# Writing out the order of the transfer queue for the whole attention stage, with a third buffer for the raw weight loads and a second one for decoded words

## The chip, the cores and the metric

The kernel runs on one core of one Trainium2 chip. The metric is device time in microseconds (us) of one execution; lower is better. Kernels are compared by the median of several executions.

The five engines have queues of their own, each worked off in order: TensorE (PE; its weight loads, PEld, overlap its matmuls), VectorE (DVE), ScalarE (ACT), GpSimd (POOL) and SyncE (SP). In this kernel nearly every DMA is issued by SP, so a DMA that has to wait for its data or for a free buffer holds up all DMAs behind it in SP's order. "Landing" is the time from a DMA's issue to the arrival of its data.

## What is computed

Three stages follow one another: an attention whose keys are masked by cluster, a dense layer with a rational activation, and a soft mixture of experts.

```python
q_assign = np.argmax(np.einsum('bhsd,hcd->bhsc', q_n, c_n), axis=-1)      # 2 x 8 heads, 768 tokens, 64 wide, 16 clusters
k_assign = np.argmax(np.einsum('bhsd,hcd->bhsc', k_n, c_n), axis=-1)
mask = q_assign[:, :, :, None] == k_assign[:, :, None, :]
scores = np.where(mask, scale * np.matmul(q, k.transpose(0, 1, 3, 2)), -1e9)
attn = softmax(scores);  x = attn @ v                                     # -> 1536 tokens x 512
h = x @ w_in                                                              # w_in 512 x 2048
g = (a0 + a1 h + a2 h^2 + a3 h^3) / (1 + |b0||h| + |b1| h^2)
y = g @ w_out                                                             # w_out 2048 x 512
out = soft_moe(y, phi, w1, w2)                                            # 8 experts, 4 slots each
```

`w_in` and `w_out` come to the core as 64-bit floats. [...]

## The kernel before

The attention works on 8 pairs of heads. A pair has 12 **slots**, one for each head and block of 128 queries, 96 slots in all (`NSL`), and a loop over the slots writes every engine's instructions out in order. In slot n PE turns the probabilities of unit n (`turn`, L349) and copies of them are made on ACT (`turned`, L355); PE computes the scores of unit n+2 (`a1_mm`, L325 and L326), DVE scales them and takes their minimum (`a1_neg`, L334), ACT exponentiates them in the next slot (`a1_exp`, L338), and PE adds some products with v (`a2_av`, L362). A unit of scores waits for a PSUM buffer that DVE's L334 of the unit before sets free, so DVE and PE follow each other closely.

Two other kinds of work are spread over the slots by a plan: a dictionary from slot to engine key to a list of functions, filled by `add(slot, steps)` and emptied by `run(slot, keys)`.

*Preparing a pair* (`prep`). The pair after next has its cluster scores computed (L216), the best cluster of every token found (L231 to L246), the masks made on ACT (`masks`, L256), k split into a high and a low part on POOL (`ksplit`, L266 and L269) and q likewise (`qsplit`, L284 and L285). The parts are then spread over operand tiles by DMAs from SBUF to SBUF: four of `ka` (L273), two of `kb` (L276), six of `qh` and `ql` (L293), eight small ones of the mask rows `nh` (L261).

*Decoding the weights* (`decode_steps`). There are 32 decodes: the even ones of blocks of `w_in`, the odd ones of `w_out`. Decode i is due at slot `DEC[i] = 2 + 53*i//20`, one in every 2.65 slots. Its steps: three slots ahead a DMA brings the raw words into `raw64[i % 2]` (L475); at slot DEC two DVE operations take them apart (`bits`, L481 and L482), the first readers of the raw words; one slot later ACT and DVE go on (L485, L488); two slots later DVE reads the raw words for the last time (`sign`, L492); three slots later POOL multiplies (`value`, L497) into `w`, of which there is one buffer. For an odd decode `w` is stored at once (L501) and PE works on it from slot +4 (L522); for an even one POOL splits it at slot +4 (`parts`, L506 and L507) and stores both parts (L508). The dense layer reads these stores back.

What sets the order: PE, ACT, DVE and POOL run in the order that the code writes out (`manual_schedule`). SP does so up to slot 12 (`SP_FREE`); from there on the scheduler of the language places SP's DMAs. Pair 1 is prepared in the first slots by a table of its own (`PREP1`, one slot for every step left in `prep`'s list).

After the attention come the dense layer (`h_mm`, L741 to L744, with weights loaded at L573) and the experts (weights loaded at L721), which the change leaves as they are.

Of the kernel before, what the change touches and what calls it, by code (L numbers as in the profile page):

```python
# [8 lines left out]
F32 = mybir.dt.float32  # L9
F32R = mybir.dt.float32r  # L10
BF16 = mybir.dt.bfloat16
I32 = mybir.dt.int32
# [40 lines left out]
def tile_kernel(ctx, tc, qT, kT, v, cenT, cenP, consts, constsb, ab, w_in, w_out, phi, w1, w2, out, dbg=None):  # L53
    nc = tc.nc
    PE, ACT, DVE, POOL, SP = nc.tensor, nc.scalar, nc.vector, nc.gpsimd, nc.sync

    B, NPB, _, S = qT.shape
    H = 2 * NPB
    D = v.shape[4]
    NP = B * H // 2  # L60
    HS = S // 2
# [50 lines left out]
    NBUF = 2  # L112

    LEAD = 2
    SP_FREE = 12

    PREP1 = (0, 0, 1, 1, 2, 3, 3, 4, 5, 6)

    OPENW = 4
    ops = [[{n: att.tile([128, S], F32R, name=f"{n}_{i}_{h}") for n in ("q1", "q2", "k1", "k2")}  # L120
# [10 lines left out]
    def load_v(p):  # L131
        b, hp = divmod(p, H // 2)
        vs[p] = v_p.tile([128, 2, 6, D], F32, tag="v", name="vt")
        SP.dma_start(vs[p], v[p])
# [6 lines left out]
    def first_pair(r, o, f):  # L141

        hold = f["hold"]
        w0 = slice(0, HS)
        ms = {}

        def q_split():
            qh, ql = (t_p.tile([128, S], F32R, tag=n, name=n) for n in ("qh", "ql"))
            hold["qh"], hold["ql"] = qh, ql
            ACT.copy(qh[:, w0], r["q"][:, w0])  # L150
            DVE.tensor_tensor(ql[:, w0], r["q"][:, w0], qh[:, w0].bitcast(F32), ALU.subtract)

        def rows(name, h):
            g = 2 * (name == "k") + h
            m = ms[name, h] = m_tile(BF16)
            oh = hold["eq"].rearrange("p i (c g) n -> p i c g n", c=2)
            for c in range(2):
                for i in range(3):
                    j = (3 * c + i) * 128
                    PE.transpose(m[64:80, j:j + 128], oh[:, i, c, g, :], identb)  # L160

        def q_rows(h, c):
            w = slice(c * HS, (c + 1) * HS)
            DVE.tensor_scalar(o[h]["q2"][64:80, w], ms["q", h][64:80, w], -1.0, None, ALU.add)

        def k_rows(h):
            ACT.activation(o[h]["k2"][64:80, :], ms["k", h][64:80, 0:S], AF.Copy, scale=BIG)

        def front(nxt):
            f["scores"]()  # L170
            q_split()
            f["ksplit"](0)
            for h in range(2):
                f["qspread"](h, w0)
            f["ksplit"](1)
            f["scaled"]()
            f["scT"]()
            f["best"](0)
            f["best"](1)
            for i in range(3):  # L180
                f["first"](i)
            idle(11)
            for h in range(2):
                rows("k", h)
                k_rows(h)
                rows("q", h)
                q_rows(h, 0)
            nxt[0]()
            idle(1)
            nxt[1]()  # L190

        def back(nxt):
            nxt[2]()
            idle(3)

        rest = [(0, "G", lambda: f["qsplit"](1)),
                (1, "D", lambda: q_rows(0, 1)),
                (2, "D", lambda: q_rows(1, 1))]
        return front, back, rest

    def prep(p):
# [3 lines left out]
        o = ops[p % NBUF]  # L205
# [47 lines left out]
        def masks():  # L253

            nh = tile_(t_p, "nh", [128, HS], F32R)
            ACT.activation(nh, hold.pop("mo")[:, 0:HS], AF.Identity, bias=cst[:, C_OFF:C_OFF + 1], scale=cst[:, C_SCL:C_SCL + 1])  # L256
            for h in range(2):
                for c in range(2):
                    w = slice(c * HS, (c + 1) * HS)
                    for n, at in (("q2", 64 * c + 16 * h), ("k2", 64 * c + 32 + 16 * h)):  # L260
                        SP.dma_start(o[h][n][64:80, w].bitcast(F32), nh[at:at + 16, :].bitcast(F32))  # L261

        def ksplit(i):
            if i == 0:
                ka, kb = tile_(t_p, "ka", [128, S], F32R), tile_(t_p, "kb", [128, S], F32R)
                POOL.tensor_scalar(ka, r["k"], 1.0, 1.0, ALU.mult, ALU.mult)  # L266
                for c in range(2):
                    w = slice(c * HS, (c + 1) * HS)
                    POOL.tensor_tensor(kb[:, w], r["k"][:, w], ka[:, w].bitcast(F32), ALU.subtract)  # L269
                for h in range(2):  # L270
                    a = slice(64 * h, 64 * h + 64)
                    for dst in (o[h]["k1"][0:64, :], o[h]["k1"][64:128, :]):
                        SP.dma_start(dst.bitcast(F32), ka[a, :].bitcast(F32))  # L273
            else:
                for h in range(2):
                    SP.dma_start(o[h]["k2"][0:64, :].bitcast(F32), hold["kb"][64 * h:64 * h + 64, :].bitcast(F32))  # L276

        def qsplit(c, done=None):
            if "qh" not in hold:
                tile_(t_p, "qh", [128, S], F32R)  # L280
                tile_(t_p, "ql", [128, S], F32R)
            qh, ql = hold["qh"], hold["ql"]
            w = slice(c * HS, (c + 1) * HS)
            POOL.tensor_scalar(qh[:, w], r["q"][:, w], 1.0, 1.0, ALU.mult, ALU.mult)  # L284
            POOL.tensor_tensor(ql[:, w], r["q"][:, w], qh[:, w].bitcast(F32), ALU.subtract)  # L285
            if c == 1:
                for h in range(2):
                    qspread(h, slice(HS, S) if p == 0 else slice(0, S))

        def qspread(h, w):  # L290
            a, l = slice(64 * h, 64 * h + 64), slice(64 - 64 * h, 128 - 64 * h)
            for dst, src in ((o[h]["q1"][a, w], hold["qh"]), (o[h]["q1"][l, w], hold["ql"]), (o[h]["q2"][0:64, w], hold["qh"])):
                SP.dma_start(dst.bitcast(F32), src[a, w].bitcast(F32))  # L293

        if p == 0:
# [6 lines left out]
            (4 + b, "D0", lambda: best(0)),  # L302
            (4 + b, "D0", lambda: best(1)),
            (5 + b, "D0", lambda: first(0)),
            (8, "G", lambda: (ksplit(0), ksplit(1))),
            (6 + b, "D0", lambda: first(1)),
            (7 + b, "D0", lambda: first(2)),
            (7 + b, "P", ohT),
            (8 + b, "A", masks),
            (11, "G", lambda: qsplit(0)),  # L310
            (12, "G", lambda: qsplit(1)),
        ]

    nvs, sums, s1s, es = {}, {}, {}, {}
# [147 lines left out]
    w_in2 = dram.tile([NF, 128, 2, NCC, 128], F32, name="w_in2")  # L462
    w_out32 = dram.tile([4, 128, 4, 512], F32, name="w_out32")

    raw64 = [dec_p.tile([128, 3, 172, 2], I32, name=f"raw64{i}") for i in range(2)]
    for t in raw64:
        POOL.memset(t.rearrange("p r n t -> p (r n t)")[:, 1024:1032], 0)

    def decode_steps(i, src, dst, after=None):

        hold = {}
        raw = raw64[i % 2]

        def dma():
            SP.dma_start(raw.rearrange("p r n t -> p (r n t)")[:, 0:1024], src)  # L475
# [17 lines left out]
                                     ALU.bitwise_and, ALU.bitwise_or)  # L493

        def value():
            w = dec_p.tile([128, 516], F32, tag="w", name="w")
            POOL.tensor_tensor(w.rearrange("p (r n) -> p r n", r=3), hold["mh"].bitcast(F32), hold["ex"].bitcast(F32),  # L497
                               ALU.mult)
            w = hold["w"] = w[:, 0:512]
            if after:  # L500
                SP.dma_start(dst, w)  # L501

        def parts():
            w = hold["w"]
            w2 = dec_p.tile([128, 2, 512], F32R, tag="w2", name="w2")
            POOL.tensor_scalar(w2[:, 0, :], w, 1.0, 1.0, ALU.mult, ALU.mult)  # L506
            POOL.tensor_tensor(w2[:, 1, :], w, w2[:, 0, :].bitcast(F32), ALU.subtract)  # L507
            SP.dma_start(dst, w2.rearrange("p a n -> p (a n)").bitcast(F32))  # L508

        return [(-3, "S", dma), (0, "D1", bits), (1, "A", expo), (1, "D1", mant), (2, "D1", sign),  # L510
                (3, "G0", value)] + (after(hold) if after else [(4, "G", parts)])

    wph = {}
    DEC = [2 + 53 * i // 20 for i in range(2 * NF)]
# [69 lines left out]
    def add(slot, steps):  # L584
        for off, eng, fn in steps:
            plan.setdefault(slot + off, {}).setdefault(eng, []).append(fn)

    def run(slot, engines):
        for eng in engines:
            for fn in plan.get(slot, {}).pop(eng, []):  # L590
                fn()
# [1 line left out]
    for g in range(2 * NP):  # L593
        add(6 * g + 6, norm(g))
    for i, d in zip(DEC, decs):
        late = i == DEC[4]
        add(i, [(max(o + (late and e == "S"), -LEAD - i), e, fn) for o, e, fn in d])
    engines = {mybir.EngineType.PE, mybir.EngineType.Activation, mybir.EngineType.DVE, mybir.EngineType.Pool}
    manual = tc.manual_schedule(engines=engines | {mybir.EngineType.SP})
    manual.__enter__()  # L600
# [11 lines left out]
    pend = None  # L612
    for n in range(-LEAD, NSL + 6):
        p, k = divmod(n, 12)
        if n == SP_FREE:
            manual.__exit__(None, None, None)
            manual = tc.manual_schedule(engines=engines)
            manual.__enter__()
        if n == -LEAD:
            run(-1, ("S",))  # L620
        if n == 0:
            run(1, ("S",))
            load_v(0)
            load(2, "k")
        if n == 1:
            load(2, "q")
        if n == 2:
            load_v(1)
        if k == 4 and n > 0 and p + 2 < NP:
            add(n, prep(p + 2))  # L630
        if k == 6 and 0 < p < NP - 1:
            load_v(p + 1)
        if n > 0 and k == 0 and p + 2 < NP and p:
            load(p + 2, "q")
# [11 lines left out]
        if n == NSL - 8:  # L646
            DVE.tensor_scalar(ncoef, coef, -1.0, None, ALU.mult)
            DVE.tensor_tensor(babs, coef[:, 4:6], ncoef[:, 4:6], ALU.max)
        run(n, ("D0", "D", "D1", "D2", "G0", "S", "G"))
        if 0 <= n < NSL:  # L650
            turn(n)
        if pend is not None:
# [665 lines left out]
```

## Time and profile before

| | |
|---|---|
| median of 3 runs | 546.82 us (545.81 to 548.43) |
| the profiled execution | 547.18 us |
| its span, first to last instruction | 545.3 us |
| attention, first to last L334 | 18.26 to 295.39 us |
| DMA engines busy, 18.26 to 269.14 us | 0.75 |

The numbers that follow come from the one profiled execution, 0.36 us above the median; 1.9 us of it lie outside its span. "Busy" is the time covered by an engine's instructions; ends of matmuls are modelled. The granted clock of TensorE (PEclk) is a share of full speed: it has two levels, 1.2 and 2.4 GHz, and 0.55 says that nearly all of a stretch went at the lower one. In the page and the answers L334 is line 334 of the kernel before.

### The profile page before, as it was taken

Reading aid. Unit: us, or ns where it says so; the run is one execution under the profiler, and the core shown is the slowest. Engines: PE = TensorE matmul, PEld = TensorE weight load, DVE = VectorE, ACT = ScalarE, POOL = GpSimd, SP = SyncE. Lnnn points to the kernel's source line nnn. Section 1 sums busy time; section 2 is a strip of 40 time slices with the busy share of each in tenths; the row PEclk is TensorE's granted clock in tenths of the full one; section 3 lists DMA queues with packets and bytes.
Section 4 is the critical chain, followed back from the end, with each engine's and each line's share of the span. In section 5 each row is a group of like instructions: output and inputs, shape, how many; then the busy total and the mean of one; then the engine's idle time right before and its main releaser. Section 6 shows DMA issues by size and latency. Waiting matters only on the chain.

```text
span 545.3 us, 9828 instructions
## 1 busy us (share of the span) xinstructions
PE 511.0 (94%) x3446; PEld 340.8 (62%) x3446; DVE 404.3 (74%) x746; ACT 362.9 (67%) x646; POOL 275.0 (50%) x315
## 2 busy tenths in 40 slices
PE   8898959989899799799999999999999999999994
PEld 3555637656556466566666687777677776765362
DVE  5678858879788588787864299999979997986022
ACT  2576746878677578678777388877678885873111
POOL 3260954945757649546542475555466544561000
PEclk9998988999989899989999999999999999999998
DMA  7988776695785777867531277766477655789997
GB/s 225 261 195 246 202 207 228 187 284 179 214 259 160 215 237 208 240 195 217 169 117 40 77 256 278 245 226 218 169 289 251 231 201 187 288 316 401 422 416 301
DMA packets 44944, 126.18 MB, mean 231 GB/s; under 512 B 7136, under 2 KB 9696, under 8 KB 40288
## 3 DMA queue, kind: packets, MB, share of 16 engines
q1 hardware_dynamic: 44752, 125.31, 70.3%
q8 instruction: 27, 0.44, 0.3%
q10 hardware_dynamic: 144, 0.26, 0.1%
q14 instruction: 21, 0.17, 0.1%
HBM read 89.56 MB, written 15.73 MB: 193 GB/s over the span
## 4 chain that ended last, share of the span: by engine, by line
PE 60%; DMA 20%; DVE 8%; SPq 5%; ACT 4%; issue 2%; POOL 0%; ACTq 0%; DVEq 0%; POOLq 0%
PE h L741 8%; PE h L744 8%; PE av L362 8%; PE h L742 8%; PE sT L349 7%; DMA raw<-w_in 5%; DMA raw<-w_out 4%; PE s L325 4%; DMA wt<-w 4%; DVE e L334 3%; PE s L326 3%; PE gt L788 3%; DMA rawk<-kT 3%; PE pf L1153 3%; SPq L261 2%
## 5 line engine op out<-in xcount | busy, mean ns | idle before, releaser
L338 ACT ACTIVATE e<-e,nv 128x768 f32<-128x768 f32 x96 | 89.9, 937 | 68.5 <-DVE e L334 62.8
L334 DVE TENSOR_SCALAR_CACHE_REDUCE e<-s 128x768 f32<-128x768 f32 x96 | 91.5, 954 | 36.0 <-PE s L326 28.4
L325 PE MATMUL s<-k,q 128*128 128x384 f32 x192 | 75.1, 391 | 18.9 <-DVE e L334 18.5
L349 PEld LDWEIGHTS sT<-cst,e 128*128 128x128 f32 x576 | 62.0, 142 | 48.8 <-ACT eT L355 23.9
L349 PE MATMUL sT<-cst,e 128*128 128x128 f32 x576 | 84.5, 283 | 3.2 <-ACT eT L355 2.7
L497 POOL TENSOR_TENSOR w<-mh,ex 128x516 f32<-128x516 f32 x32 | 41.2, 1286 | 87.1 <-DVE ex L492 32.4
L355 ACT COPY eT<-sT 128x768 f32<-128x768 f32 x96 | 75.3, 784 | 11.4 <-PE sT L349 11.2
L741 PE MATMUL h<-xh,w 128*128 128x512 f32 x192 | 80.6, 420 | 0.4 <-DMA w<-w_in 0.4
L362 PE MATMUL av<-eT,vt 128*64 128x384 f32 x384 | 80.7, 524 | 0.0
L742 PE MATMUL h<-xl,w 128*128 128x512 f32 x192 | 75.3, 392 | 0.0
L758 POOL TENSOR_SCALAR q<-u,babs 128x512 f32<-128x512 f32 x47 | 36.2, 771 | 74.5 <-ACT u L756 74.5
L326 PE MATMUL s<-k,q 80*128 80x384 f32 x192 | 66.8, 348 | 0.8 <-DMA k<-kb 0.6
L760 POOL TENSOR_TENSOR q<-q,u 128x512 f32<-128x512 f32 x47 | 60.9, 1296 | 3.8
L744 PE MATMUL h<-xh,w 128*128 128x512 f32 x192 | 52.9, 396 | 0.0
L325 PEld LDWEIGHTS s<-k,q 128*128 128x128 f32 x192 | 37.1, 193 | 24.7 <-DVE e L334 24.1
L756 ACT ACTIVATE u<-h 128x512 f32<-128x512 f32 x47 | 27.9, 594 | 28.5 <-PE h L744 28.1
L741 PEld LDWEIGHTS h<-xh,w 128*128 128x128 f32 x192 | 36.1, 188 | 16.9 <-DVE r L774 6.7
L759 DVE TENSOR_TENSOR p<-p,h 128x512 f32<-128x512 f32 x47 | 32.1, 683 | 15.0 <-ACT p L757 14.9
L744 PEld LDWEIGHTS h<-xh,w 128*128 128x128 f32 x192 | 36.0, 188 | 8.5
L742 PEld LDWEIGHTS h<-xl,w 128*128 128x128 f32 x192 | 36.2, 189 | 6.8 <-issue 0.5
L481 DVE TENSOR_SCALAR ex<-raw 128x516 int32<-128x516 int32 x32 | 21.8, 681 | 23.0 <-DMA raw<-w_in 11.3
L766 ACT ACTIVATE r<-q,epsc 128x512 f32<-128x512 f32 x47 | 32.8, 698 | 9.0 <-POOL q L760 7.4
(198 smaller groups left out, 950.5 us busy)
## 6 DMA issues: line engine op xcount, KB each, us to landing
wt<-w SPq DMA_DIRECT2D x32, 1024.0 KB, 7.5
w<-w_in SPq DMA_DIRECT2D x96, 256.0 KB, 3.3
raw<-w_in SPq DMA_DIRECT2D x16, 512.0 KB, 5.3
raw<-w_out SPq DMA_DIRECT2D x16, 512.0 KB, 4.5
w_in<-w SPq DMA_DIRECT2D x16, 512.0 KB, 3.1
k<-ka SPq DMA_DIRECT2D x32, 192.0 KB, 3.8
q<-qh SPq DMA_DIRECT2D x28, 192.0 KB, 4.8
w_out<-w SPq DMA_DIRECT2D x16, 256.0 KB, 4.5
```

The source lines that it names most:

```text
L325: PE.matmul(ps[:, c, 0:HS], o["q1"][:, it], o["k1"][:, w], start=True, stop=False)
L326: PE.matmul(ps[:, c, 0:HS], o["q2"][0:80, it], o["k2"][0:80, w], start=False, stop=True)
L334: DVE.tensor_scalar(e, s1s.pop(u)[:, :, 0:HS], -(D ** -0.5), None, ALU.mult, ALU.min, accum_out=nvs[g][:, rest:rest + 1])
L338: ACT.activation(es[u], es[u], AF.Exp, scale=-1.0, bias=nvs[g][:, rest:rest + 1], accum_out=sums[g][:, rest:rest + 1])
L349: PE.transpose(ps[:, j // 3, j % 3 * 128:(j % 3 + 1) * 128], e[:, j, :], ident)
L355: ACT.copy(dst, eTp.pop(u)[:, :, 0:HS].rearrange("p c (j t) -> p c j t", j=3))
L362: PE.matmul(av[g][64 * h:64 * h + 64, 0:HS], vs[g // 2][:, h, j, :], eTs[g][:, h, j, :], start=(j == 0), stop=(j == 5))
L497: POOL.tensor_tensor(w.rearrange("p (r n) -> p r n", r=3), hold["mh"].bitcast(F32), hold["ex"].bitcast(F32), ALU.mult)
L741: PE.matmul(h, wh[:, c, :], xh[t][:, c, :], start=(c == 0), stop=False)
L742: PE.matmul(h, wh[:, c, :], xl[t][:, c, :], start=False, stop=False)
L744: PE.matmul(h, wl[:, c, :], xh[t][:, c, :], start=False, stop=(c == NCC - 1))
L760: POOL.tensor_tensor(q, q, u, ALU.mult)
```

## The change

In the attention SP is now in the written order up to its end, and every DMA has a slot of its own. Within a slot the raw loads (key "L") come first, then loads of v, q and k, then all stores (key "S"), which stand at least one slot behind the step that makes their data (the k stores one and two slots, the mask rows two). Raw loads are due four slots ahead, not three, and there are three raw buffers; `w` has two buffers. The loads of v(0), q(2), k(2) and v(1) get other slots. No arithmetic changes.

```diff
-    SP_FREE = 12
-    PREP1 = (0, 0, 1, 1, 2, 3, 3, 4, 5, 6)
+    PREP1 = (0, 0, 1, 1, 2, 3, 3, 4, 5, 6, 2, 3, 5, 7)
...
@@ prep: the steps of a pair
-            (8, "G", lambda: (ksplit(0), ksplit(1))),
+            (8, "G", lambda: ksplit(0)),
...
             (11, "G", lambda: qsplit(0)),
             (12, "G", lambda: qsplit(1)),
+            (9, "S", lambda: ksplit(1)),
+            (10, "S", lambda: ksplit(2)),
+            (10 + b, "S", mspread),
+            (13, "S", qspreads),
...
@@ decode_steps
-    raw64 = [dec_p.tile([128, 3, 172, 2], I32, name=f"raw64{i}") for i in range(2)]
+    NRAW = 3
+    raw64 = [dec_p.tile([128, 3, 172, 2], I32, name=f"raw64{i}") for i in range(NRAW)]
...
-        raw = raw64[i % 2]
+        raw = raw64[i % NRAW]
...
-            w = dec_p.tile([128, 516], F32, tag="w", name="w")
+            w = dec_p.tile([128, 516], F32, tag="w", name="w", bufs=2)
...
-            if after:
-                SP.dma_start(dst, w)
...
-            SP.dma_start(dst, w2.rearrange("p a n -> p (a n)").bitcast(F32))
+            hold["w2"] = w2.rearrange("p a n -> p (a n)").bitcast(F32)
-
-        return [(-3, "S", dma), (0, "D1", bits), (1, "A", expo), (1, "D1", mant), (2, "D1", sign),
-                (3, "G0", value)] + (after(hold) if after else [(4, "G", parts)])
+        def store():
+            SP.dma_start(dst, hold["w" if after else "w2"])
+
+        return [(-4, "L", dma), (0, "D1", bits), (1, "A", expo), (1, "D1", mant), (2, "D1", sign),
+                (3, "G0", value)] + ([(4, "S", store)] + after(hold) if after else [(4, "G", parts), (5, "S", store)])
...
@@ the loop over slots
-        if n == SP_FREE:
-            manual.__exit__(None, None, None)
-            manual = tc.manual_schedule(engines=engines)
-            manual.__enter__()
-        if n == -LEAD:
-            run(-1, ("S",))
-        if n == 0:
-            run(1, ("S",))
+        run(n, ("L",))
+        if n == 1:
             load_v(0)
+        if n == 2:
             load(2, "k")
-        if n == 1:
+        if n == 3:
             load(2, "q")
-        if n == 2:
+        if n == 8:
             load_v(1)
...
-        if k == 6 and 0 < p < NP - 1:
+        if k == 8 and 0 < p < NP - 1:
             load_v(p + 1)
...
-        run(n, ("D0", "D", "D1", "D2", "G0", "S", "G"))
+        run(n, ("S", "D0", "D", "D1", "D2", "G0", "G"))
```

`ksplit(1)` now issues the four stores of `ka`, `ksplit(2)` the two of `kb`, `mspread` the eight of `nh` and `qspreads` the six of `qh` and `ql`.

PE and ACT keep their instructions and their order; one small DVE operation and one small POOL operation change places with a neighbour, and POOL clears the tail of the third raw buffer once at the start. What moves is SP's order, shown at two places.

**SP, the preparation of pair 2** (the raw loads are numbered by buffer: `raw_140` is the first). Before, with the six decodes 0 to 5 loaded or about to be:

```order
L475 DMA raw_140<-w_in 128x1024
L508 DMA w_in_138<-w_667 128x1024
L475 DMA raw_141<-w_out 128x1024
L501 DMA w_out_139<-w 128x512
L273 DMA k_0_0_119<-ka 64x768 x2
L276 DMA k_0_0_120<-kb 64x768
L129 DMA rawk<-kT 128x768
L261 DMA q_0_0_118<-nh 16x384
L475 DMA raw_140<-w_in 128x1024
L508 DMA w_in_138<-w_845 128x1024
L293 DMA q_0_0_117<-qh 64x768
L475 DMA raw_141<-w_out 128x1024
```

Now:

```order
L486 DMA raw_142<-w_out 128x1024
L127 DMA rawq<-qT 128x768
L520 DMA w_in_138<-w_670 128x1024
L486 DMA raw_140<-w_in 128x1024
L127 DMA rawk<-kT 128x768
L520 DMA w_out_139<-w 128x512
L278 DMA k_0_0_119<-ka 64x768 x2
L281 DMA k_0_0_120<-kb 64x768
L264 DMA q_0_0_118<-nh 16x384
L486 DMA raw_141<-w_out 128x1024
L520 DMA w_in_138<-w_845 128x1024
L299 DMA q_0_0_117<-qh 64x768
```

Of each group of k, mask and q stores only the first row is shown. The load of decode 6 (the second `raw_140` before, the `raw_140` now) stood behind the stores of k and of the mask rows and now stands ahead of them; decode 7 takes its old place (`raw_141` now), and the load of rawk has gone ahead of the stores as well.

**SP, the preparation of pair 1, in slots 1 to 9.** Before:

```order
L129 DMA rawk<-kT 128x768
L129 DMA rawq<-qT 128x768
L273 DMA k_1_0_127<-ka 64x768 x2
L276 DMA k_1_0_128<-kb 64x768
L134 DMA vt<-v 128x768
L475 DMA raw_140<-w_in 128x1024
L261 DMA q_1_0_126<-nh 16x384
L475 DMA raw_141<-w_out 128x1024
L508 DMA w_in_138<-w_502 128x1024
L293 DMA q_1_0_125<-qh 64x768
```

Now:

```order
L127 DMA rawk<-kT 128x768
L278 DMA k_1_0_127<-ka 64x768 x2
L486 DMA raw_142<-w_in 128x1024
L127 DMA rawq<-qT 128x768
L281 DMA k_1_0_128<-kb 64x768
L486 DMA raw_140<-w_out 128x1024
L264 DMA q_1_0_126<-nh 16x384
L520 DMA w_in_138<-w_502 128x1024
L299 DMA q_1_0_125<-qh 64x768
```

The loads of decodes 2 and 3 (`raw_140` and `raw_141` before, `raw_142` and `raw_140` now) have both gone ahead of the mask rows; the six q stores come behind the same store of `w_in` as before, and the load of v(1) now follows them.

## Rows read from the trace of the kernel before

**Rows 1.** The page, section 1: busy time of each engine over the span.

```profile
PE 511.0 (94%) x3446; PEld 340.8 (62%) x3446; DVE 404.3 (74%) x746; ACT 362.9 (67%) x646; POOL 275.0 (50%) x315
```

**Rows 2.** Windows: stretch, length, busy time per engine, PEclk, DMA share, GB/s.

```profile
18.26:269.14 250.88, 228.91 (x1471) 149.21 (x1471) 198.23 (x370) 180.42 (x321) 149.16 (x171) 0.96 0.75 219
237.04:269.14 32.10, 31.83 (x211) 20.86 (x210) 26.83 (x48) 25.56 (x47) 20.68 (x25) 1.00 0.75 219
```

**Rows 3.** Line L481: what its engine sat idle for (us, times).

```profile
  DMA raw<-w_in: 11.3, 3
  DMA raw<-w_out: 10.5, 4
  POOL ql L285: 1.2, 1
```

**Rows 4.** Timeline, 60 to 79 us (start, duration, instruction, idle before it).

```profile
60.37 2.57 SPq L273 DMA_DIRECT2D k<-ka  x4
...
69.55 1.10 DVE L492 SCALAR_TENSOR_TENSOR ex<-raw,ex 128x516 int32<-128x516 int32 x1
...
71.78 0.53 SPq L475 DMA_DIRECT2D raw<-w_in  x1
...
76.28 0.69 DVE L481 TENSOR_SCALAR ex<-raw 128x516 int32<-128x516 int32 x1 [5.63 <-DMA raw<-w_in]
...
78.49 0.69 PE L325 MATMUL s<-k,q 128*128 128x384 f32 x1 [5.46 <-DVE e L334]
```

**Rows 5.** Windows around five waits of L481, columns as in rows 2.

```profile
37.00:43.00 6.00, 3.64 (x28) 2.06 (x24) 2.79 (x8) 2.31 (x4) 2.79 (x4) 1.00 0.31 67
43.00:47.20 4.20, 4.11 (x16) 2.49 (x16) 2.98 (x8) 3.29 (x6) 0.00 (x0) 0.59 0.95 318
69.50:78.40 8.90, 3.44 (x23) 1.64 (x22) 3.27 (x8) 2.09 (x4) 3.99 (x5) 0.97 0.66 193
78.40:85.20 6.80, 6.71 (x26) 4.99 (x27) 3.66 (x9) 4.53 (x8) 3.12 (x5) 0.54 1.04 293
144.00:149.00 5.00, 3.06 (x23) 1.24 (x22) 2.33 (x4) 1.61 (x4) 1.49 (x2) 1.00 1.01 292
149.00:153.00 4.00, 3.81 (x19) 1.82 (x20) 2.75 (x9) 3.72 (x7) 3.66 (x7) 0.57 1.01 255
179.50:183.30 3.80, 0.95 (x9) 0.64 (x6) 2.21 (x5) 0.51 (x2) 1.22 (x1) 1.00 0.94 363
183.30:187.50 4.20, 4.20 (x24) 1.76 (x24) 2.80 (x6) 3.63 (x7) 3.95 (x6) 0.59 0.50 115
...
231.00:235.00 4.00, 3.96 (x15) 2.47 (x16) 3.56 (x8) 3.37 (x6) 0.00 (x0) 0.57 0.32 131
```

**Rows 6.** Waits of SP's queue: line, releaser, us in total, times, longest.

```profile
SPq L508 <- POOL w L507: 43.1, 9, 8.1
SPq L475 <- DVE ex L492: 30.4, 12, 5.6
```

**Rows 7.** Line L475, the raw loads: time from issue to landing.

```profile
DMA to landing us min/median/max: 3.3/5.1/7.5
```

**Rows 8.** Timeline and chain, 40 to 51 us: the operands of pair 1.

```profile
40.88 0.69 DVE L481 TENSOR_SCALAR ex<-raw 128x516 int32<-128x516 int32 x1 [3.21 <-DMA raw<-w_in]
41.48 0.53 SPq L475 DMA_DIRECT2D raw<-w_out  x1
...
42.57 0.51 SPq L293 DMA_DIRECT2D q<-qh  x1
...
44.40 6.31 DMA q<-qh
50.75 0.45 PE L326 MATMUL s<-k,q 80*128 80x384 f32 x1 [0.23 <-DMA q<-qh]
```

**Rows 9.** Timeline: the last store of the decode and the dense layer's first matmul.

```profile
279.50 0.32 SPq L501 DMA_DIRECT2D w_out<-w  x1
...
300.41 0.50 PE L741 MATMUL h<-xh,w 128*128 128x512 f32 x1
```

More of the change, by code (lines that the diff above doesn't have):

```diff
@@ L172, in front @@
             f["ksplit"](0)
+            f["ksplit"](1)
             for h in range(2):
                 f["qspread"](h, w0)
-            f["ksplit"](1)
+            f["ksplit"](2)
             f["scaled"]()
@@ L196, in first_pair @@
         rest = [(0, "G", lambda: f["qsplit"](1)),
+                (1, "S", lambda: f["qspreads"](slice(HS, S))),
                 (1, "D", lambda: q_rows(0, 1)),
@@ L256, in masks, with mspread @@
             ACT.activation(nh, hold.pop("mo")[:, 0:HS], AF.Identity, bias=cst[:, C_OFF:C_OFF + 1], scale=cst[:, C_SCL:C_SCL + 1])
+        def mspread():
+            nh = hold["nh"]
             for h in range(2):
@@ L269, in ksplit @@
                     POOL.tensor_tensor(kb[:, w], r["k"][:, w], ka[:, w].bitcast(F32), ALU.subtract)
+            elif i == 1:
+                ka = hold["ka"]
                 for h in range(2):
@@ L285, in qsplit, with qspreads @@
             POOL.tensor_tensor(ql[:, w], r["q"][:, w], qh[:, w].bitcast(F32), ALU.subtract)
-            if c == 1:
-                for h in range(2):
-                    qspread(h, slice(HS, S) if p == 0 else slice(0, S))
+        def qspreads(w=slice(0, S)):
+            for h in range(2):
+                qspread(h, w)
         def qspread(h, w):
@@ L495, in value @@
         def value():
-            w = dec_p.tile([128, 516], F32, tag="w", name="w")
+            w = dec_p.tile([128, 516], F32, tag="w", name="w", bufs=2)
             POOL.tensor_tensor(w.rearrange("p (r n) -> p r n", r=3), hold["mh"].bitcast(F32), hold["ex"].bitcast(F32),
                                ALU.mult)
-            w = hold["w"] = w[:, 0:512]
-            if after:
-                SP.dma_start(dst, w)
+            hold["w"] = w[:, 0:512]
         def parts():
@@ L595, in tile_kernel @@
     for i, d in zip(DEC, decs):
-        late = i == DEC[4]
-        add(i, [(max(o + (late and e == "S"), -LEAD - i), e, fn) for o, e, fn in d])
+        add(i, [(max(o, -LEAD - i), e, fn) for o, e, fn in d])
     engines = {mybir.EngineType.PE, mybir.EngineType.Activation, mybir.EngineType.DVE, mybir.EngineType.Pool}
```

## The prediction

> **What bounds the kernel now.** I read the page first: PE is busy for 511.0 of 545.3 us [rows 1], so what can be won lies where PE is not busy, or slow. Windows over the attention find that place. From the first scaling of pair 0 to that of pair 7, seven pairs, 250.88 us pass with PE busy for 228.91 at a mean granted clock of 0.96; the last of the seven pairs takes 32.10 us with PE busy for 31.83 at 1.00 [rows 2]. At that pace seven pairs would take 7 x 32.10 = 224.7 us, so 26.2 us are lost somewhere in the first six.
>
> The answer for one line says where. L481, the first DVE operation that reads raw weight words, had DVE idle for 11.3 + 10.5 us before it because a raw load had not landed, in seven places, and 1.2 us in an eighth, named after POOL, which I count with them [rows 3]: **23.0 us in eight waits**. A decode is no work that anybody is in a hurry for, but L481 stands in DVE's queue ahead of the next scaling of scores (L334), and PE can't start new scores until that has freed its buffer.
>
> The timeline shows the worst of them. SP begins to issue the k stores of a pair at 60.37, goes on through k, rawk and the mask rows, and only at 71.78 comes to the raw load that stands behind them. DVE had finished the previous decode at 70.65 (69.55 + 1.10); L481 starts at 76.28, after 5.63 us of idle time, and PE's next scores start at 78.49 after 5.46 [rows 4]. So the load is late because it is issued late, behind 15 DMAs that take 71.78 - 60.37 = 11.4 us to issue.
>
> A wait has a sequel. In five of the eight places the clock is at 0.54 to 0.59 in the 4 to 7 us behind it, that is nearly all at 1.2 GHz, with PE busy for 95% of the time or more; in the stretch of the wait itself, where PE did little, it still reads 0.97 to 1.00 [rows 5].
>
> What makes SP late are also its own waits: 43.1 us for POOL's second part of a w_in block, in nine waits of up to 8.1, and 30.4 us for DVE's last read of a raw buffer (L492), in twelve [rows 6]. Everything behind such a DMA waits with it.
>
> **The change, part by part.** All sums are against the profiled execution (547.18 us, 0.36 above the median of the runs).
>
> *Raw loads one decode earlier, third buffer.* A load at slot DEC - 4 needs the last read of its buffer three decodes before, which is at slot DEC - 7.95 + 2, two slots earlier. So the wait for L492 [rows 6] should go. More important is the place in the queue: in the order of pair 2 the load behind the mask rows is now decode 7's, not 6's. A decode is due 2.65 slots after the one before, and a slot lasts 32.10 / 12 = 2.675 us [rows 2], so each load stands some 7.1 us earlier against its need. The longest wait is 5.63 [rows 4]. I checked what stands behind a burst now. Issuing from the first k store to the end of the mask rows takes 11.4 us, 10.7 without rawk, which has gone ahead: four slots. If SP starts it at its own slot (13 for pair 2), decode 7's load goes out in slot 17; its bits are read in slot 20, 8.0 us later, and a landing takes 5.1 us in the median, 7.5 at the most [rows 7]. No wait remains, with 0.5 to 2.9 us in hand. The sum gets **-23.0**.
>
> *The clock behind the waits.* At full clock the PE work of the five low stretches is worth its busy time times its clock: 6.71 x 0.54 + 4.11 x 0.59 + 3.81 x 0.57 + 4.20 x 0.59 + 3.96 x 0.57 = 12.9 us, in place of their 23.2 us [rows 5]. That is 10.2 us, if PE alone sets the pace there. The other bound is 0: DVE and ACT are busy for 54 to 93% of those stretches and can't be hurried much. Against the undisturbed pair, 26.2 are lost in all, which leaves 3.2 beside the 23.0. I take the middle of 3.2 and 10.2, rounded down: **-6.0**.
>
> *Operands of pair 1.* Here the change takes less than it uncovers. At present the q stores begin at 42.57, one transfer issued at 44.40 takes 6.31 us, and PE's second matmul of pair 1 starts at 50.75, 0.23 us late for it [rows 8]. So q is already just in time. Without the wait of 3.21 at 40.88 [rows 8], and with the stretch behind it at full clock (4.20 - 4.11 x 0.59 = 1.8 us [rows 5]), PE would be there 5.0 us earlier. The q stores move up only by the two raw loads that leave the queue ahead of them, about 0.6 us each by the row of one: 0.53 us, and its gap [rows 8]. A new wait of 5.0 - 1.2 = **+3.8** on q; bounds 0 (POOL and the masks let SP run further ahead) and 5.0. For later pairs the q stores stand at slot 13 of their preparation and are needed five slots or 13.4 us later, against a longest landing of 6.31 here: nothing.
>
> *Stores a slot later.* SP comes to a store when its data should be there, so most of the 43.1 us of waits [rows 6] turn into issuing. That moves no engine by itself; it is what keeps the loads at their slots, and is counted above. The parts of a w_in block have one buffer, filled again 5.3 slots or 14.2 us later: cover enough for a store a slot later. The last store, at 279.50, is read back by the dense layer, whose first matmul is at 300.41 [rows 9]; a slot, 2.7 us, fits into those 20.9.
>
> *Second buffer for w.* POOL no longer waits for a w_out store before it can write the next w. POOL is at 149.16 of 250.88 us [rows 2]; its result goes to a store and, one slot later, to PE or to its own next step. Counted at nothing; if POOL ran late, the store behind it would hold SP, which is the last rival.
>
> *Loads of v, q, k in other slots, one more clearing of a buffer tail on POOL at the start, two neighbours swapped.* All are covered by slots of 2.7 us ahead of their readers. Nothing.
>
> *What stays late.* The loads now crowd differently, so one or the other may still arrive after its reader: 0 to 5.6 us, the longest wait of today. I take **+1.0**.
>
> Sum: -23.0 - 6.0 + 3.8 + 1.0 = -24.2; 547.2 - 24.2 = **523.0 us**. What follows the attention, from the dense layer's first matmul at 300.41 [rows 9] to the end of the span of 545.3, is 244.9 us long and moves up as it is. By the bounds: 547.2 - 23.0 - 10.2 = 514.0, and 547.2 - 23.0 + 5.0 + 5.6 = 534.8.
>
> **The rivals.**
>
> *The DMA engines are full, not the queue late.* Two of the four stretches with a wait in rows 5 show the DMA engines at 1.01 and 0.94 of their time, two at 0.31 and 0.66 [rows 5]. In a full stretch an earlier issue only puts the raw load among other transfers. If half the loads keep their waits, the gain is (23.0 + 6.0) / 2 = 14.5, less 3.8 for q: 547.2 - 10.7 = 536.5. Against it: over the seven pairs the engines are busy for 0.75 of the time [rows 2], and an earlier load can use the rest. The Trainium skill states the ground for this rival (DMA: Bandwidth & Descriptors, Issuing engines are not separate DMA queues): all DMAs end on the same 16 engines and interleave there, so an order of issue adds no bandwidth. By that rule alone the time would be this rival's 536.5. The trace agrees in the stretches at 1.01 and 0.94 and not in the others.
>
> *The clock comes back whole and q is in time.* Then the lower bound holds, 514.0. For it: PE is busy nearly all the time behind the waits; against it, the single undisturbed pair.
>
> *The change doesn't do what it says.* The loads are late behind SP's issuing itself, 11.4 us a burst, and four slots of lead are eaten by it: about 547. The order speaks against it, since the late ones are ahead of the burst now.
>
> *The written order holds the loads up.* SP can no longer pass a store whose data is late, and a raw load follows each w_in store closely. Today SP waits for POOL there up to 8.1 us [rows 6]. A late load costs (23.0 + 6.0) / 8 = 3.6 us. If POOL's part came so late that a load arrived after its reader in 7 decodes of 32, the gain less q (25.2) would be gone; from there on it is slower. A third of the decodes, 11, gives 547.2 - 25.2 + 11 x 3.6 = 561.6. The deciding point is a store more than 10.7 - 5.1 = 5.6 us behind its slot. For it: the 8.1. Against it: a slot of 2.7 us has been added, and POOL is idle two fifths of the time.
>
> **How the numbers follow.** Forecast 0.60; full engines 0.17; full clock 0.08; no effect 0.06; held up 0.09. A measurement of this kernel can tell about 0.5%, 2.7 us. Faster: 0.60 + 0.17 + 0.08 = 0.85; same 0.06; slower 0.09. The range goes from just below the lower bound, 513, to just above the case of full engines, 539, and leaves out 0.15 and the tails.
>
> **What would show it.** Right: L481 waits for raw loads below 4 us in all; SP's wait for L492 is gone; the seven pairs take 225 to 230 us at a clock of 0.98 or more; PE waits 2 to 5 us for q at the first unit of pair 1. Wrong: raw waits of over 10 us in all, with the DMA engines full beside them (full engines) or SP standing at a w_in or w_out store for POOL beforehand (held up); or raw waits gone and the seven pairs still at 250 us, with a new releaser ahead of L334.

## The result and the profile after

The changed kernel takes **520.01 us** in the median of four runs (518.78 to 522.36), the kernel before 547.62 on the same chip: ratio 0.9505, 95% interval 0.9459 to 0.9552. The forecast was 523.0, the range 513 to 539. The profiled execution took 518.78 us, 28.4 less than the one of before; all but 1.0 us of that lies in the attention.

The lines have moved. What was L481 (DVE reads the raw words, the 64-bit weights as pairs of 32-bit words) is now L492, L492 (DVE's last read of a raw buffer) is L503, L475 (the raw loads) L486, L497 (POOL makes `w`) L508, L507 (POOL's second part of a w_in block) L516; L334 is L344, L325 and L326 are L335 and L336, L741 is L747, and all stores of decoded words go out from L520. Experiments built on the kernel before keep the old numbers.

The page, section 1, where [rows 1] stood:

```profile
PE 501.1 (97%) x3446; PEld 336.0 (65%) x3446; DVE 404.5 (78%) x746; ACT 362.7 (70%) x646; POOL 274.3 (53%) x316
```

Windows, columns as in [rows 2]: the seven pairs, and the last of them.

```profile
18.32:241.80 223.48, 219.13 (x1471) 144.54 (x1471) 198.64 (x371) 180.24 (x321) 148.37 (x171) 1.00 0.84 246
210.05:241.80 31.75, 31.32 (x208) 20.62 (x205) 27.12 (x50) 25.36 (x46) 21.35 (x27) 1.00 0.73 218
```

The seven pairs went from 250.88 to 223.48 us, 27.4 less. The last pair, which had no wait before, gained 0.35. So the others came down to its pace, 32.0 us in the mean of the six. PE gives the same 27.4 in two parts: 9.8 us less busy (228.91 to 219.13), with the same number of matmuls at a clock of 1.00 in place of 0.96, and 17.6 us less idle (21.97 to 4.35). The DMA engines move the same bytes in less time: share 0.84, before 0.75.

The answer for L492, where [rows 3] stood (first and last start, then what its engine sat idle for before it):

```profile
L492 DVE TENSOR_SCALAR ex<-raw x32: 646/680/690, 25.3 to 245.5; 128x516 int32<-128x516 int32 x32
...
its engine sat idle before it (us, times) until:
who waited for it (us, times):
```

The list is empty: the 23.0 us are gone, to the last.

The timeline at the places of [rows 4], [rows 8] and [rows 9], with one row of the chain (44 us):

```profile
40.88 0.50 SPq L299 DMA_DIRECT2D q<-qh  x1
...
43.93 3.77 DMA q<-ql
...
47.70 0.42 PE L336 MATMUL s<-k,q 80*128 80x384 f32 x1 [0.48 <-DMA q<-ql]
48.57 0.94 DVE L344 TENSOR_SCALAR_CACHE_REDUCE e<-s 128x768 f32<-128x768 f32 x1
...
55.23 2.85 SPq L278 DMA_DIRECT2D k<-ka  x4
...
65.49 0.53 SPq L486 DMA_DIRECT2D raw<-w_out  x1
...
67.34 0.68 DVE L492 TENSOR_SCALAR ex<-raw 128x516 int32<-128x516 int32 x1
...
273.07 0.50 PE L747 MATMUL h<-xh,w 128*128 128x512 f32 x1
```

The burst of pair 2 begins at 55.23 and its load follows at 65.49, 10.3 us later. But that load is decode 7's now, which is read 9.4 us after its issue, at 74.91; the bits read at 67.34 are decode 6's, long landed. The dense layer starts at 273.07 in place of 300.41.

Waits of SP, and the landing of L486:

```profile
SPq L486 <- DVE ex L503: 28.2, 14, 5.2
SPq L520 <- POOL w L516: 25.5, 8, 8.1
SPq L520 <- POOL w L508: 12.2, 7, 4.9
```

```profile
DMA to landing us min/median/max: 3.4/5.4/9.0
```

SP still waits, for DVE and for POOL, nearly as long as in [rows 6]. It does so early now: from a load's issue to L492's read of it 13.9 us pass in the median and 7.7 at the least, against 7.5 and 3.6 before (from the 32 pairs of starts in the timeline).

And POOL no longer waits for a store of `w`. In the kernel before its L497 idled for such stores, in four places:

```profile
  DMA w_out<-w: 20.7, 4
```

### The profile page after: what moved, and what is told of

It reads as the page before. It is cut to its first block, busy times and chain, and to the rows that moved or that the text cites. A ratio compares the mean times of both kernels' runs of the same rounds, so it can differ in the third digit from the quotient of the medians.

```text
span 517.0 us, 9835 instructions
## 1 busy us (share of the span) xinstructions
PE 501.1 (97%) x3446; PEld 336.0 (65%) x3446; DVE 404.5 (78%) x746; ACT 362.7 (70%) x646; POOL 274.3 (53%) x316
## 4 chain that ended last, share of the span: by engine, by line
PE 67%; DMA 13%; DVE 9%; ACT 5%; SPq 2%; issue 1%; POOL 1%; ACTq 0%; DVEq 0%
PE h L747 9%; PE av L372 9%; PE sT L359 9%; PE h L750 9%; PE h L748 9%; DMA wt<-w 7%; PE s L335 5%; PE s L336 4%; DVE e L344 4%; PE gt L794 4%; DMA raw<-w_out 3%; ACT e L348 2%; PE l L806 2%; SPq L299 2%; ACT eT L365 2%; DMA w_in<-w 1%
## 5 line engine op out<-in xcount | busy, mean ns | idle before, releaser
L344 DVE TENSOR_SCALAR_CACHE_REDUCE e<-s 128x768 f32<-128x768 f32 x96 | 91.5, 954 | 32.9 <-PE s L336 25.6
L747 PE MATMUL h<-xh,w 128*128 128x512 f32 x192 | 80.6, 420 | 0.0
L372 PE MATMUL av<-eT,vt 128*64 128x384 f32 x384 | 77.2, 504 | 0.0
L508 POOL TENSOR_TENSOR w<-mh,ex 128x516 f32<-128x516 f32 x32 | 41.2, 1287 | 64.5 <-DVE ex L503 44.9
L335 PE MATMUL s<-k,q 128*128 128x384 f32 x192 | 73.5, 383 | 1.7 <-DVE e L344 1.5
L336 PE MATMUL s<-k,q 80*128 80x384 f32 x192 | 65.1, 339 | 1.1 <-DMA k<-kb 0.6
L747 PEld LDWEIGHTS h<-xh,w 128*128 128x128 f32 x192 | 36.1, 188 | 16.2 <-DVE r L780 4.2
L335 PEld LDWEIGHTS s<-k,q 128*128 128x128 f32 x192 | 36.4, 189 | 6.7 <-DVE e L344 5.9
L336 PEld LDWEIGHTS s<-k,q 80*128 80x128 f32 x192 | 36.6, 190 | 1.8 <-issue 1.1
```

The lines of the kernel that those rows point to most:

```text
L335: PE.matmul(ps[:, c, 0:HS], o["q1"][:, it], o["k1"][:, w], start=True, stop=False)
L336: PE.matmul(ps[:, c, 0:HS], o["q2"][0:80, it], o["k2"][0:80, w], start=False, stop=True)
L344: DVE.tensor_scalar(e, s1s.pop(u)[:, :, 0:HS], -(D ** -0.5), None, ALU.mult, ALU.min, accum_out=nvs[g][:, rest:rest + 1])
L372: PE.matmul(av[g][64 * h:64 * h + 64, 0:HS], vs[g // 2][:, h, j, :], eTs[g][:, h, j, :], start=(j == 0), stop=(j == 5))
L747: PE.matmul(h, wh[:, c, :], xh[t][:, c, :], start=(c == 0), stop=False)
```

## The experiments

All ratios are to the kernel before on the same chip, with a 95% interval; where two medians are set against each other in us, they can be of different chips. "W" is the idle time of DVE ahead of its first read of raw words, as in [rows 3]: 23.0 us before, 0 now.

**The third buffer and the earlier load alone**, on the kernel before:

```diff
-    raw64 = [dec_p.tile([128, 3, 172, 2], I32, name=f"raw64{i}") for i in range(2)]
+    raw64 = [dec_p.tile([128, 3, 172, 2], I32, name=f"raw64{i}") for i in range(3)]
-        raw = raw64[i % 2]
+        raw = raw64[i % 3]
-        return [(-3, "S", dma), (0, "D1", bits),
+        return [(-4, "S", dma), (0, "D1", bits),
```

> The kernel before with a third raw buffer and the raw loads due four slots ahead, and nothing else: SP's order is still the scheduler's after slot 12, stores are issued where they were, w has one buffer. Theory (place of the load): what counts is that each raw load stands one decode earlier in SP's queue; the scheduler, with a third buffer, puts decode 6's load ahead of the k stores of pair 2 as well. L481 waits for raw loads 0 to 4 us in all, 519 to 526 us. Rival (written order): the loads are late because of the scheduler's order and of stores issued too soon; L481 still waits 12 us or more and the time is 535 or more.

Measured: 532.81 us, 0.976 (0.9703 to 0.9818), half the gain and in neither expectation. The answers for L481 and for POOL's waits:

```profile
  DMA raw<-w_in: 3.0, 1
  POOL w L497: 2.6, 2
  DMA raw<-w_out: 0.9, 1
```

```profile
POOL w L497 <- DMA w_out<-w: 38.3, 7, 9.3
...
PE mf L522 <- POOL w L497: 4.6, 5, 1.8
...
DVE ex L481 <- POOL w L497: 2.6, 2, 2.2
```

W fell from 23.0 to 6.5, and 2.6 of that is POOL. (The profile is of the slowest of the four executions, 537.97 us, so its waits are at the upper end.) POOL waits 38.3 us for stores of `w`, up to 9.3 at a time, before it can write the next `w`; then PE's use of `w` (mf) and DVE's next decode wait for POOL. So the loads were not all of it.

**The same with the second buffer for `w`** (`name="w", bufs=2` besides).

> The kernel with the third raw buffer and the lead of four slots alone (532.8 us), and now the second w buffer too; order and slots of the stores as before the change. Theory (w): what that kernel lacked is w: POOL there waits 38.3 us for w_out stores, in seven waits, and arrives late for DVE and PE. With two w buffers these waits go, and the time is 519 to 525. Rival (order): w is off the path, the rest of the gain is the written order with its later stores; the time stays at 530 to 535.

Measured: 525.74 us, 0.9631 (0.9565 to 0.9697): 7.1 us better than without `w`. W is 0.8 us in the profile, which is of the fastest of the four executions, 522.04 us. Here, in the old order of the queue, the wait for q at pair 1 that I had forecast is seen in the timeline:

```profile
49.21 0.41 PE L325 MATMUL s<-k,q 128*128 128x384 f32 x1 [2.99 <-DMA q<-ql]
...
49.99 0.44 PE L326 MATMUL s<-k,q 80*128 80x384 f32 x1 [0.37 <-DMA q<-qh]
...
50.84 0.96 DVE L334 TENSOR_SCALAR_CACHE_REDUCE e<-s 128x768 f32<-128x768 f32 x1 [3.16 <-PE s L326]
```

PE waits 2.99 and 0.37 us for q, DVE idles 3.16 us for those scores, and the first pair takes 32.82 us, against 30.25 in the changed kernel.

**The second buffer for `w` alone**, on the kernel before.

> The kernel before with a second w buffer and nothing else. Theory (one wait hides the other): while raw loads are late, POOL's waits for w_out stores (20.7 us in four) lie beside them; without these the raw waits stay at 17 to 26 us and the time at 541 to 549. Rival (w is worth its 10 us by itself, as it is in the changed kernel): 531 to 539.

Measured: 536.11 us, 0.9823 (0.9772 to 0.9874): 10.7 us from one buffer. L481, SP's wait for POOL, and the seven pairs:

```profile
  DMA raw<-w_out: 8.1, 4
  DMA raw<-w_in: 5.7, 3
  POOL w L497: 3.2, 2
```

```profile
SPq L508 <- POOL w L507: 26.2, 7, 8.1
```

```profile
17.79:254.88 237.09, 221.56 (x1471) 145.37 (x1471) 194.53 (x370) 179.74 (x321) 147.03 (x171) 0.99 0.78 232
```

The theory that one wait only hides the other fell. With two `w` SP stands 26.2 us for POOL instead of 43.1 [rows 6], the raw loads queued behind those stores are late by less, W falls to 17.0 and its longest wait from 5.63 to 3.12 us. The pairs gain more than these 6.0 us: PE is idle for 6.4 us less and busy for 7.4 us less, at a clock of 0.99 in place of 0.96. In W the two buffers add up: 16.5 us from the one, 6.0 from the other, 22.2 from both.

**One `w` in the changed kernel.**

```diff
-            w = dec_p.tile([128, 516], F32, tag="w", name="w", bufs=2)
+            w = dec_p.tile([128, 516], F32, tag="w", name="w")
```

> The changed kernel with one w buffer. Theory (w): POOL waits for each w_out store again, which now even starts a slot later: 30 us of such waits or more, DVE waits for POOL, 528 to 540. Rival (w off the path, as the prediction counted it): 518 to 523.

Measured: 535.58 us, 0.9806 (0.972 to 0.9893), 15.6 us over the changed kernel's 520.01. L508 (what POOL idled for, and who waited for it):

```profile
  DMA w_out<-w: 39.4, 8
...
who waited for it (us, times):
  PEld mf L534: 4.2, 3
  DVE ex L492: 3.8, 2
  PE mf L534: 3.3, 2
```

No raw load is late here, and the time is lost all the same: POOL waits for stores, up to 13.89 us at a time, PE and DVE for POOL. The seven pairs take 239.5 us with PE busy for 225.3, at a clock of 0.98.

**Two raw buffers in the changed kernel**, as it stands (`NRAW = 2`).

> The changed kernel with two raw buffers in place of three; order, lead of four slots and the second w stay. Theory (place): a load now waits in SP's queue for the last read two decodes before, at slot DEC - 3.3, some 0.7 slots or 1.9 us after its own slot, and then has 8.8 us to land; it still stands ahead of the bursts, so L481 waits 0 to 6 us in all and the time is 520 to 529. Rival (buffer): the third buffer is the gain; with two, L481 waits 15 us or more and the time is 538 to 547.

Measured: 604.1 us, 1.1041 (1.0993 to 1.109). A load four slots ahead is written into the order before the last reads of a buffer that only two decodes share, so this kernel computes part of its decodes from the words of the block two later, and DVE waits for those:

```profile
DVE mh L499 <- DMA raw<-w_in: 40.9, 10, 9.1
```

It says nothing about the buffer, only what a load asked for too late costs. The question went to the next kernel.

**Two raw buffers, loads three slots ahead and behind those reads.**

```diff
-    NRAW = 3
+    NRAW = 2
-        return [(-4, "L", dma), (0, "D1", bits),
+        return [(-3, "SL", dma), (0, "D1", bits),
-        run(n, ("S", "D0", "D", "D1", "D2", "G0", "G"))
+        run(n, ("S", "D0", "D", "D1", "D2", "G0", "SL", "G"))
```

> The changed kernel with two raw buffers, the loads three slots ahead and written behind the slot's DVE and POOL work as in the kernel before, so that the reads of the buffer's last words stay ahead of the load. Order, later stores and second w stay. Theory (place): decode 6's load now stands behind the k stores and ahead of the mask rows, between the place before and the place of the changed kernel, so L481's counterpart waits 4 to 14 us in all, and 524 to 534 us. Rival (buffer): without the third buffer nothing is won, 538 or more.

Measured: 536.34 us, 0.9831 (0.9753 to 0.9908), between the two expectations and nearer the rival's. L492, and the seven pairs:

```profile
  DMA raw<-w_out: 10.0, 4
  DMA raw<-w_in: 5.4, 1
```

```profile
18.22:259.80 241.58, 225.41 (x1470) 148.37 (x1471) 195.09 (x371) 180.41 (x321) 147.43 (x171) 0.97 0.79 227
```

Here written order, later stores and second `w` together bring no more than `w` alone (0.9823) as long as there are two raw buffers. In exchange for the third buffer SP waits 50.7 us for DVE's last reads, and W is 15.4.

**The scheduler orders SP again from slot 12 on**, the rest as changed.

```diff
+        if n == 12:
+            manual.__exit__(None, None, None)
+            manual = tc.manual_schedule(engines=engines)
+            manual.__enter__()
         run(n, ("L",))
```

> The changed kernel with SP given back to the scheduler at slot 12, as before; buffers, leads and slots of the stores stay. Theory (place): the loads stay one decode ahead, so 518 to 523 us and no wait of L481 above 1 us. Rival (written order): 530 us or more, with raw waits back behind the bursts.

Measured: 520.99 us, 0.9525 (0.9482 to 0.9567), W 0.6: no difference to the changed kernel that can be told.

**Every store back in the slot that makes its data**, issued at that slot's end.

```diff
-            (9, "S", lambda: ksplit(1)),
+            (8, "S9", lambda: ksplit(1)),
-            (13, "S", qspreads),
+            (12, "S9", qspreads),
...
-                (3, "G0", value)] + ([(4, "S", store)] + after(hold) if after else [(4, "G", parts), (5, "S", store)])
+                (3, "G0", value)] + ([(3, "S9", store)] + after(hold) if after else [(4, "G", parts), (4, "S9", store)])
...
+        run(n, ("S9",))
```

> The changed kernel with every store back in the slot that makes its data (the last thing of that slot), in SP's written order; buffers and lead stay. Theory (place): SP stands longer at the stores (for POOL 35 us or more in all, 25.5 + 12.2 in the changed kernel), but the lead of four slots covers it: 518 to 524 us, L481 waits below 3 us in all. Rival (held up): the waits at the stores pass on to the loads behind them; L481 waits 8 us or more, 530 us or more.

Measured: 522.71 us, 0.9553 (0.9512 to 0.9593), W 1.8. The later stores are worth 0 to 2.7 us, no more than can be told.

**Loads two slots ahead, and one**, in place of four.

> The changed kernel with the raw loads two slots ahead instead of four; three buffers. Price of a late load: two slots are 5.3 us, a landing takes 5.4 in the median, so loads behind a burst arrive late: raw waits of 8 to 30 us in all, W. Theory (a wait costs more than itself, by the clock behind it): 520 plus 1.26 W, with a mean clock over the span below 0.99. Rival (a wait costs itself): 520 plus W or less.

> The changed kernel with the raw loads one slot ahead instead of four; three buffers. One slot is 2.7 us, a landing takes 5.4, so nearly every one of 32 decodes waits: raw waits W of 60 to 130 us. Theory (long waits cost more than themselves, by the clock behind them; short ones less): a mean clock of the attention below 0.96 and 520 + 1.1 to 1.3 W. Rival (a wait costs itself or less, whatever its length): 520 + 0.8 to 1.0 W, clock 0.97 or more.

```diff
-        return [(-4, "L", dma), (0, "D1", bits),
+        return [(-2, "L", dma), (0, "D1", bits),
```

(-1 in the second.) Measured: 529.2 us, 0.9709 (0.9653 to 0.9766), with two; 544.67 us, 0.9958 (0.9928 to 0.9988), with one. L492 and the seven pairs of the first, then of the second:

```profile
  DMA raw<-w_out: 6.5, 3
  DMA raw<-w_in: 1.6, 2
```

```profile
20.88:250.92 230.04, 220.26 (x1470) 145.18 (x1471) 195.97 (x371) 180.13 (x321) 147.65 (x171) 1.00 0.81 239
```

```profile
  DMA raw<-w_out: 15.0, 7
  DMA raw<-w_in: 8.2, 5
  POOL s L381: 1.8, 1
```

```profile
20.05:267.29 247.24, 224.95 (x1471) 147.38 (x1471) 194.27 (x370) 179.71 (x321) 145.99 (x171) 0.98 0.75 222
```

W grows as the lead shrinks: 0 with four slots, 8.1 with two, 25.0 with one. With two the time lies between what the expectations give for this W (530.2 and 528.1), and part of it is no wait of L492: the first scaling comes at 20.88 in place of 18.32. With one it is the rival's, 540 to 545. The lead is what the third buffer is for; with one slot of it nearly the whole gain is gone, whatever the rest of the change does. I had expected far more of a lead of one, since a slot is 2.7 us. But a slot is a place in the queue and no time: where nothing holds SP it runs ahead of the other engines, and these loads still go out 6.8 us before their read in the median.

## Why the prediction was right, and where not

- **What bounds.** Right as to the place, and in part as to the cause. With the raw waits gone PE is busy for 219.13 of 223.48 us (said: 225 to 230). But the late loads were not the whole loss of the six pairs: with one `w` no raw load is late, and 15.6 us are lost.
- **Raw waits, -23.0.** The size is right, and the mechanism is seen: what stands behind the burst is the next decode's load, with the burst at 10.3 us (said: 10.7), the read 9.4 us behind the load (said: 8.0), and the lead experiments as the test. But I booked all of it, and the clock behind it, on the third buffer and the lead, and these alone left W at 6.5 us and gave 14.4 of the 29.0.
- **Clock, -6.0.** Right in size as I defined it: 27.4 less the 23.0, with 0.5 spent on q, leaves 4.9. It is a remainder, not measured by itself. PE's own account puts more on the clock and less on the waits: 9.8 us of busy time, close to the upper bound of 10.2, and 17.6 of idle time. Before, PE was idle for 21.97 us in all, so the 23.0 of DVE could not all have been PE's.
- **Operands of pair 1, +3.8.** The mechanism held, the size didn't. PE waits 0.48 us for q, in one place (said: 3.8), and the first unit of pair 1 comes at 48.57 in place of 51.59: 3.0 earlier, where my terms gave 1.2. The q stores begin at 40.88, not 42.57, so 1.7 earlier and not 1.2, and the one that PE waited for landed in 3.77 us, where I had kept today's 6.31. In the old order, with both buffers, the wait is there: 2.99 and 0.37 us.
- **What stays late, +1.0.** Nothing did. And 1.0 us went after the attention, where I had said that all moves up as it is.
- **SP's wait for the last raw read "should go".** It did not: 28.2 us, before 30.4. SP gets to the load that much sooner, and after its wait there are still 7.7 us or more from issue to read. A wait of a queue says nothing of its cost until one sees what stands behind it.
- **The step that failed: the second buffer for `w`, "counted at nothing".** I argued from POOL's busy share (149.16 of 250.88 us) that it had time. It had, but could not use it, since it stood for a store in SP's queue; the 20.7 us of that wait were in the trace of before, and I did not use them. `w` is worth 10.7 us alone and 15.6 when taken out of the changed kernel. The sum came out within 3 us for all that because I had put the whole loss on the loads, and each of the two causes made part of the same W: the buffer and lead alone give 2.4%, `w` alone 1.8%, both 3.7%, the whole change 4.95%. That was luck: without the second `w` in the change the sum would have been the same 523.0, and 532.81 and 535.58 us are measured without it.
- **The rest, 1.3%,** is what the order of the queue brings beside the buffers. In the profiled executions the seven pairs differ by 3.2 us (226.68 against 223.48), and 2.6 of them are the first pair (32.82 against 30.25); the medians are 5.7 apart, and what makes the rest of that was not seen. With SP in the scheduler's hands after slot 12 nothing is lost, and with early stores at most 2.7 us. How the remainder is shared between the other slots was not tried.
- **Rivals.** Full engines: fell. At a DMA share of 0.84 no load is late, though a landing takes longer than before (5.4 us in the median, 9.0 at most). The same bytes are moved (219 GB/s over 250.88 us, 246 over 223.48), and landings got no shorter (median 5.1 before). The page's rule is that DMAs end on the same 16 engines and interleave there, whichever engine issues them (the Trainium skill, DMA: Bandwidth & Descriptors, Issuing engines are not separate DMA queues); nothing here goes against it. That an order of issue gains nothing, and so 536.5, was my conclusion, and it fell: the engines had idle time that earlier issues could use. Held up: SP still stands for POOL, 25.5 + 12.2 us with up to 8.1 at a time, beyond the 5.6 that I gave as the deciding point, and no load is late; with 13.9 us from issue to read that point was set too near, and a wait of 8.1 us need not be a store 8.1 us late, since SP can reach it ahead of its slot. Full clock with q in time, 514.0: in kind nearly this, 6 us too low. No effect: fell.

## What to carry to other kernels

Where one in-order queue carries both loads and stores, the lead of a load has to cover the longest burst and wait ahead of it plus its landing, and it needs the buffers for that. Whether it does shows in the time from issue to first use, not in slots. An engine that is idle half of the time can still lie on the path, if a single buffer ties it to a store in that queue: ask of each single buffer who must finish before it is written again, and who waits for that engine then. One wait can be fed by two causes, and then its size does not say what either is worth: try each alone and each taken out.

## What the runs showed of the chip that I had not expected

A microsecond of waiting did not cost the same in every kernel. For five of them, the seven pairs less the 223.48 us of the changed one, taken apart by PE's busy and idle time in the windows (longest wait from the timeline):

| kernel | W us | longest wait us | clock | more idle us | more busy us | in all, per us of W |
|---|---|---|---|---|---|---|
| lead of two | 8.1 | 3.1 | 1.00 | 5.4 | 1.1 | 0.81 |
| second `w` alone | 17.0 | 3.1 | 0.99 | 11.2 | 2.4 | 0.80 |
| lead of one | 25.0 | 3.2 | 0.98 | 17.9 | 5.8 | 0.95 |
| two raw buffers | 15.4 | 5.4 | 0.97 | 11.8 | 6.3 | 1.18 |
| before | 23.0 | 5.6 | 0.96 | 17.6 | 9.8 | 1.19 |

PE's idle time is 0.66 to 0.77 of W in all five. What differs is the busy time that comes on top at the lower of the clock's two levels: 0.14, 0.14 and 0.23 us for each us of W in the first three, 0.41 and 0.43 in the last two. So W of 25.0 us cost less with a lead of one (23.8 us) than 23.0 in the kernel before (27.4), which also has only one `w`.

The table suggests that the longest wait decides, 3.2 us or less against 5.4 and 5.6, but it does not. The kernel with one `w` in the changed order has W of 3.8 us, its longest wait of L492 is 2.4, and its PE is busy for 6.2 us more. Windows show where the clock falls (lead of two, lead of one, one `w`):

```profile
20.88:23.00 2.12, 2.12 (x7) 1.45 (x7) 1.80 (x3) 1.03 (x2) 1.42 (x2) 0.52 0.98 269
23.00:250.92 227.92, 218.14 (x1465) 143.74 (x1465) 194.17 (x369) 179.11 (x319) 146.23 (x169) 1.00 0.81 238
```

```profile
54.00:60.00 6.00, 6.00 (x42) 4.07 (x43) 5.05 (x10) 5.00 (x9) 2.48 (x4) 1.00 0.45 174
182.00:186.00 4.00, 4.00 (x25) 1.28 (x23) 2.64 (x6) 3.36 (x7) 0.00 (x0) 0.57 1.02 224
```

```profile
57.70:63.90 6.20, 6.15 (x21) 4.27 (x22) 4.22 (x5) 4.46 (x8) 5.96 (x7) 0.50 0.86 261
```

With a lead of two it is low at the start of the stretch alone, ahead of all waits of L492, and 1.00 behind the five of them; so nearly all of the 1.1 us of that kernel are no price of W. Nor are most of the 2.4 us with the second `w` alone, where it falls only once, to 0.67 from 47.8 to 53.0, behind 1.10 and 0.36 us of PE waiting for q. With a lead of one PE was idle for 3.06 us until 53.98 and then ran at 1.00, and for 2.64 us until 181.69 and then ran at 0.57. So the busy time on top comes with the waits behind which the clock falls, five of eight in the kernel before and three of thirteen with a lead of one, and not with W as such. What decides behind which wait it falls, these runs do not show.
